# Output products of an attention and SwiGLU block over three PSUM banks instead of two, and turns of h in the bank that stands idle

## The chip, the cores and the metric

The kernel runs on one core of one Trainium2 chip. The metric is the device time of one execution in microseconds, taken as the median of several runs. The profile is one more execution, recorded by the hardware profiler. Its times are counted from the start of its span.

## The reference

One block of a transformer with conditioned layer norms is computed, for 2048 rows of 576 columns. Six vectors of shift, gain and gate come from a condition `c`. Attention has 32 query heads over 16 key and value heads; of the 2048 keys only the last 512 are used, and nothing is masked. The MLP has 4608 inner columns.

```python
mod = (_silu(c) @ w_mod).reshape(c.shape[0], 6, 1, -1)
h = _layernorm(x) * (1 + ca) + sa
q = (h @ wq).reshape(B, Sq, 32, 128).transpose(0, 2, 1, 3)
p = _softmax(einsum("bhqd,bhkd->bhqk", q, k[:, :, -512:]) * 128 ** -0.5)
o = einsum("bhqk,bhkd->bhqd", p, v[:, :, -512:])
x = x + ga * (o.transpose(0, 2, 1, 3).reshape(B, Sq, 4096) @ wo)
h = _layernorm(x) * (1 + cb) + sb
out = x + gb * ((_silu(h @ w1) * (h @ w3)) @ w2)
```

## The kernel before

All engines run in an order that the Python code writes out itself. Each product is made of f16 halves (a high part and a low part), three matmuls for one.

Attention goes through 128 slots, one for a query head and a block of 512 rows; the index is `i`. A slot has four steps `t`, one for 128 of its rows, so a step (i, t) is the unit of the order. In a step TensorE makes the scores of 128 rows against 512 keys (`scores`, L513, three matmuls of 512 columns into tile `pss`), a third of the next slot's query (`query`, L440 and L444, into `pq`; none at t = 3), and one piece of an older pair's output product. At t = 1 it also turns the last quarter of the slot before (`turn`, L554, into `pt`), and after t = 3 it multiplies the slot before by its values (`values`, L593, twelve matmuls into `po`). VectorE finds the exponents (L517), ScalarE takes the exponential (L531) and GpSimd the low halves (L568). The other three quarters of each slot are turned by DMA.

The output product of a pair of heads is `attend_out`. Each of four row tiles of 128 rows is one unit: `back` (L463) is called for head 0 in one step and for head 1 in the next, each time with six matmuls of 128x288, and after the second VectorE adds the sum to the residual: `acc` (L623, 128x576, one instruction over both halves). Units begin at even t and end at odd t. All units of the attention stage use the same two PSUM banks, the tile `E` (in the profile `pe`), columns 0 to 287 of each; small sums over peaks stand in columns 400 to 416 of its second bank (L333, L338, L1174, L1180).

PSUM has eight banks of 512 f32 columns: two for tag A (`pq`, `po`, in the MLP `py`), two for S (`pss`, `px`), two for `E`, two for T (`pt`). The T banks hold the turned quarter of each slot, and now and then a turn of normalised rows (`turn_rows`, L258, four transposes into one bank): those of h for the blocks 1, 2 and 3 before their first use (`make_h`, read by ScalarE in `modulate`, L267, L269, L271, L273), and those of the second norm's h for the blocks 0 and 1 (`store_h`, read by ScalarE, L662). `make_h` runs for blocks 2 and 3 at the steps (8, 0), (8, 1), (8, 2), (9, 0), (9, 1) and (11, 0) to (12, 1); `store_h` runs at (112, 0) to (113, 1) and (115, 0) to (116, 1) in the same pattern. Two rows of shift and gain (`mod_cols`, L170) and a scaling (`scale_cols`, L1108, at (110, 1)) also use T, and the gates (`mod_rows`, L182) use `E`. Tasks of a step (`run(i, t)`) come after its piece of output product.

Block 1's h is made during the first slot (`make_h` with `early`), block 0's ahead of it (`modulate_first`, L285 and L287, from five turned banks, two of them T). The first query goes into `E` (`project_first`, L450 to L456).

When attention ends, the T banks are given back and become a second pair `pf`; from then on `pe` and `pf` take turns (`lane`). The MLP has 72 groups of seven products (L880) and the down products (L965, added by VectorE at L959).

The waits between engines are put in by the tile framework from the tiles that each instruction names.

Of the kernel before, what the change touches and what calls it, by code (L numbers as in the profile page):

```python
# [20 lines left out]
P = 128  # L21
D = 576
DC = 4
# [25 lines left out]
def tile_block(  # L49
# [30 lines left out]

    E = psum.tile([P, 2, 512], F32, tag="E", name="pe", bufs=1)
    turning = ExitStack()
    tpool = turning.enter_context(tc.tile_pool(name="tpool", bufs=2, space=PSUM))

    def t_bank():
        return tpool.tile([P, 512], F32, tag="T", name="pt")

# [73 lines left out]
    def mod_cols(wm, name, one, tag):  # L161

        ps = t_bank() if tag == "T" else bank(tag, f"ps_{name}")
# [12 lines left out]
    def mod_rows(wm, kind):  # L176

        vec = gate_rows[kind]
        wm = wm[0]
        for h in range(2):  # L180
            for d in (0, 3):
                nc.tensor.matmul(  # L182
                    E[:, h, :HALF], ones, wm[:, d, h * HALF : (h + 1) * HALF], start=d == 0, stop=d == 3
                )
        nc.vector.tensor_copy(half_split(vec), E[:, :, :HALF])
        return vec
# [67 lines left out]
    def turn_rows(b, m, tag):  # L254

        ps = t_bank() if tag == "T" else bank(tag, "ps_n")
        for t in range(ST):
            nc.tensor.transpose(ps[:, t * P : (t + 1) * P], norms[b][1][t][:, m * P : (m + 1) * P], ident)  # L258
        return ps
# [70 lines left out]
    def sum_peaks(g, lo, hi, ps=None):  # L330

        ps = E[:, 1, 400:416] if ps is None else ps
        nc.tensor.matmul(ps[:, lo:hi], peak_ones, tops[g][:, lo:hi], start=True, stop=True)  # L333

    def take_sums(g, lo, hi, ps=None):

        ps = E[:, 1, 400:416] if ps is None else ps
        nc.vector.tensor_copy(peaks[g][:, 5 + lo : 5 + hi], ps[:, lo:hi])  # L338
# [118 lines left out]

    def back(ps, o, w, t, first, last):

        rows = slice(t * P, (t + 1) * P)  # L460
        for n, (x, y) in enumerate(((0, 0), (0, 1), (1, 0))):
            for h in range(2):
                nc.tensor.matmul(  # L463
                    ps[:, h, :HALF],
                    o[:, x, rows],
                    w[:, y, h * HALF : (h + 1) * HALF],
                    start=first and n == 0,
                    stop=last and n == 2,
                )

    QP = (range(0, 5), range(5, 10), range(10, 14))
# [13 lines left out]
    def query(i, part):  # L485
        u, j, b = slots[i]
        st = state[i]
        if part == 0 or i == 0:
            st["q"] = bank("A", "pq") if i else E[:, 0, :]
        ps = st["q"]  # L490
        if i == 0:
            project_first(ps, wqs[u, j], hT[b])
        else:
            project(ps, wqs[u, j], hT[b], QP[part])
        if part == len(QP) - 1:
            q = st["qT"] = pool.tile([P, 2, SB], F16, tag=("qh", "ql")[i % 2], name="qT", bufs=QB)
# [51 lines left out]
    def turn(i, t):  # L548

        st = state[i]  # L550
        p = st.pop(("p", t))
        ps = st["t"] = t_bank().rearrange("p (j n) -> p j n", j=KC)
        for j in range(KC):
# [60 lines left out]

    def attend_out(pair, t, j, total):
        u, _, b = slots[2 * pair]
        lane[0] += j == 0
        ps = spare()
        back(ps, state[2 * pair + j]["o"], wos[u][:, j], t, j == 0, j == 1)
        if j == 1:  # L620
            run(*total)
            a = half_split(acc[b][:, t, :])
            nc.vector.scalar_tensor_tensor(  # L623
                a, ps[:, :, :HALF], factors[:, uses[u][0], 2:3], a, op0=ALU.mult, op1=ALU.add
            )
# [29 lines left out]
    def store_h(b, m, tag, tag_out):  # L655
# [8 lines left out]
        )  # L664
        store_later(hd[b][m * P : m * P + n, :], hf[:n], ("s", b, m) if tag == "T" else None)

# [266 lines left out]
    def down(d, u):  # L933

        pair = d // G
        lane[0] += 1
        ps = lane[1][lane[0] % 2]
        if u < 4:
# [28 lines left out]
    def plain(j, i, t):  # L967

        d = 2 * G - 1
        lane[0] += 1  # L970
        ps = lane[1][lane[0] % 2]
        w = osets[d, 3 if j else 4]
# [181 lines left out]

    lane = [0, ()]

    def spare():
        return lane[1][lane[0] % 2] if lane[1] else E

    def in_peak(f, part):  # L1160
# [8 lines left out]
    def in_total(f):  # L1169

        m = peak_cols[:, 4 * (f % 2) :][:, :4]
        for part in range(2):
            peak = m[:, 2 * part + 1 : 2 * part + 2]
            nc.tensor.matmul(  # L1174
                spare()[:, 1, 408:410], peak.to_broadcast([P, P]), m[:, 2 * part : 2 * part + 2],
                start=part == 0, stop=part == 1,
            )

    def in_taken(f):
        nc.vector.tensor_copy(stats[:, f, :], spare()[:, 1, 408:410])  # L1180

# [23 lines left out]
    def out_total(p):  # L1205
        nc.tensor.matmul(spare()[:, 1, 410:411], peak_ones, peak_cols[:, 8 + p % 2 : 9 + p % 2], start=True, stop=True)

    def out_taken(p):
        nc.vector.tensor_copy(out_down[:, p : p + 1], spare()[:, 1, 410:411])

# [235 lines left out]
    def make_h(b, m, early=False):  # L1446
        modulate(hT[b], m, turn_rows(b, m, "T"), vecs["shift", "a"], vecs["gain", "a"], early)

# [86 lines left out]
    at(14, 2, lambda: scale_gate("b", mlp_small, mlp_gate_down))  # L1535
    at(106, 2, make_cols, "shift", "b", 3, 0.0, "T")
    at(109, 2, make_cols, "gain", "b", 4, 1.0, "T")
# [71 lines left out]
    for i in range(n + 2):  # L1609
        run(i, -1)  # L1610
        for t in range(ST):
# [121 lines left out]
```

## Time and profile before

| | |
|---|---|
| median of 3 runs | 2750.64 us (2748.8 to 2751.75) |
| the profiled execution: its own time | 2750.74 us |
| its span on the core | 2748.9 us |
| mean granted TensorE clock | 0.997 |
| TensorE matmul busy | 2678.7 us |
| VectorE, ScalarE, GpSimd busy | 1943.0, 1622.0, 1874.0 us |
| attention, from the first to the last output product | 89 to 1616 us |

PE is TensorE's matmuls, PEld its weight loads, DVE VectorE, ACT ScalarE, POOL GpSimd, SP the engine whose queue issues most DMAs. A group's row gives the line, engine and operation, the tiles out<-in, the shapes and the count, then busy microseconds and mean nanoseconds of one, then the idle time of the engine just ahead of them and what ended it. In the timeline a row begins with its start and its length. A wait's row gives the total, how often, and the longest.

### The profile page before, as it was taken

Reading aid. Unit: us, or ns where it says so; the run is one execution under the profiler, and the core shown is the slowest. Engines: PE = TensorE matmul, PEld = TensorE weight load, DVE = VectorE, ACT = ScalarE, POOL = GpSimd, SP = SyncE. Lnnn points to the kernel's source line nnn. Section 1 sums busy time; section 2 is a strip of 40 time slices with the busy share of each in tenths; the row PEclk is TensorE's granted clock in tenths of the full one; section 3 lists DMA queues with packets and bytes.
Section 4 is the critical chain, followed back from the end, with each engine's and each line's share of the span. In section 5 each row is a group of like instructions: output and inputs, shape, how many; then the busy total and the mean of one; then the engine's idle time right before and its main releaser. Section 6 shows DMA issues by size and latency. Waiting matters only on the chain. (4 is left out here: it accounts for less than half of the span.)

```text
span 2748.9 us, 45218 instructions
## 1 busy us (share of the span) xinstructions
PE 2678.7 (97%) x15406; PEld 1510.3 (55%) x15406; DVE 1943.0 (71%) x3582; ACT 1622.0 (59%) x3026; POOL 1874.0 (68%) x1747
## 2 busy tenths in 40 slices
PE   6899999999999999999999999999999999999998
PEld 3455555555555555555555555555555555555555
DVE  7876777777777777877765567777776666566566
ACT  6776778777777778787677635544443333333332
POOL 4677888888888877877669536688874455333435
PEclk9999999999999999999999999999999999999999
DMA  6888888788787878879879945656643444333332
GB/s 200 184 175 196 184 182 186 176 188 187 167 181 170 190 186 211 200 179 212 187 192 226 224 137 169 201 168 200 209 151 111 153 122 128 106 102 112 104 109 81
DMA packets 593463, 463.87 MB, mean 169 GB/s; under 512 B 442704, under 2 KB 472528, under 8 KB 592208
## 3 DMA queue, kind: packets, MB, share of 16 engines
q1 hardware_dynamic: 592944, 460.69, 66.1%
q8 instruction: 121, 1.98, 0.3%
q14 instruction: 110, 0.90, 0.1%
q10 hardware_dynamic: 288, 0.30, 0.0%
HBM read 264.19 MB, written 95.99 MB: 131 GB/s over the span
## 5 line engine op out<-in xcount | busy, mean ns | idle before, releaser
L568 POOL TENSOR_TENSOR hp<-p,hp 128x512 f16<-128x512 f32 x384 | 447.6, 1168 | 267.0 <-ACT hp L563 154.5
L531 ACT ACTIVATE p<-pss,table,factors 128x512 f32<-128x512 f32 x512 | 396.8, 775 | 351.2 <-DVE table L517 182.4
L517 DVE CUSTOM_DVE_ANT_0 spent<-pss,factors 128x512 uint8<-128x512 f32 x512 | 381.2, 745 | 237.6 <-PE pss L513 236.2
L880 PEld LDWEIGHTS <-wset 128*128 128x128 f16 x3528 | 344.2, 98 | 337.2 <-issue 3.7
L880 PE MATMUL py<-hset,wset 128*128 128x512 f16 x2016 | 482.1, 379 | 0.0
L463 PE MATMUL pe<-o 128*128 128x288 f16 x3024 | 453.0, 286 | 10.6 <-DVE acc L623 10.3
L513 PE MATMUL pss<-k,qT 128*128 128x512 f16 x1536 | 417.7, 380 | 15.3 <-ACT p L531 13.0
L463 PEld LDWEIGHTS <-o 128*128 128x128 f16 x3072 | 300.4, 98 | 184.8 <-issue 16.3
L593 PE MATMUL po<-ptw,v 128*128 128x512 f16 x1536 | 357.1, 381 | 8.8 <-DMA ptw<-hp 2.7
L880 PE MATMUL px<-hset,wset 128*128 128x512 f16 x1512 | 361.5, 379 | 2.2 <-ACT p L531 2.2
L94 POOL TENSOR_TENSOR akv<-u,akv 128x512 f16<-128x512 f32 x141 | 165.2, 1181 | 178.0 <-ACT akv L93 170.2
L440 PE MATMUL pq<-hT,wq 128*128 128x512 f16 x1092 | 280.5, 379 | 0.0
L563 ACT CAST hp<-p 128x512 f16<-128x512 f32 x384 | 237.4, 618 | 15.5 <-DMA ptw<-hp 2.3
L593 PEld LDWEIGHTS <-v 128*128 128x128 f16 x1536 | 147.6, 98 | 174.6 <-issue 13.0
L513 PEld LDWEIGHTS <-qT 128*128 128x128 f16 x1536 | 147.3, 98 | 129.3 <-issue 17.4
L965 PEld LDWEIGHTS <-akv 128*128 128x128 f16 x1728 | 169.0, 98 | 89.3 <-issue 0.7
L623 DVE SCALAR_TENSOR_TENSOR acc<-pe,factors,acc 128x576 f32<-128x576 f32 x252 | 204.2, 810 | 13.0 <-PE pe L463 5.1
L613 POOL TENSOR_TENSOR o<-on,o 128x512 f16<-128x512 f32 x128 | 149.7, 1170 | 54.6 <-ACT o L612 52.2
L440 PEld LDWEIGHTS <-wq 128*128 128x128 f16 x1092 | 106.9, 98 | 127.2 <-issue 1.0
L959 DVE SCALAR_TENSOR_TENSOR acc<-pf,table,acc 128x576 f32<-128x576 f32 x140 | 113.5, 811 | 79.3 <-PE pf L965 79.3
L1058 ACT COPY u<-py 128x512 f32<-128x512 f32 x72 | 42.2, 586 | 200.8 <-PE py L880 198.8
L1051 ACT ACTIVATE s<-s,table 128x512 f32<-128x512 f32 x72 | 52.0, 722 | 175.6 <-DVE s L1050 175.6
(254 smaller groups left out, 4734.2 us busy)
## 6 DMA issues: line engine op xcount, KB each, us to landing
wset<-wd SPq DMA_DIRECT2D x213, 320.0 KB, 3.2
r<-row SPq DMA_DIRECT2D x128, 256.0 KB, 3.9
oset<-od SPq DMA_DIRECT2D x106, 288.0 KB, 3.2
wraw<-in_w SPq DMA_DIRECT2D x36, 768.0 KB, 5.4
wd<-wmade SPq DMA_DIRECT2D x75, 320.0 KB, 3.5
wset<-wd SPq DMA_DIRECT2D x71, 160.0 KB, 2.2
w2raw<-in_w SPq DMA_DIRECT2D x19, 576.0 KB, 5.2
wd<-ring SPq DMA_DIRECT2D x33, 320.0 KB, 2.7
```

The source lines that it names most:

```text
L94: eng.tensor_sub(halves[:, 1], src, halves[:, 0])
L440: nc.tensor.matmul(ps, w[:, k // 2, m, :], hT[:, DC + m if k == 1 else m, :], start=s == 0, stop=False)
L463: nc.tensor.matmul(ps[:, h, :HALF], o[:, x, rows], w[:, y, h * HALF : (h + 1) * HALF], start=first and n == 0, stop=last and n == 2,)
L513: nc.tensor.matmul(pss, q[:, x, rows], k[:, y, :], start=n == 0, stop=n == 2)
L517: nc.vector.tensor_tensor_reduce(spent, pss, to_log.to_broadcast([P, W]), turned, 3.0e38, op0=ALU.add, op1=ALU.min, accum_out=nm)
L531: nc.scalar.activation(p, pss, AF.Exp, bias=nm, scale=factor, accum_out=st["l"][:, t : t + 1])
L563: nc.scalar.copy(hp[:, 0, :], state[i]["p", t])
L568: nc.gpsimd.tensor_sub(hp[:, 1, :], state[i].pop(("p", t)), hp[:, 0, :])
L593: nc.tensor.matmul(po, v[:, x, c, :], pt[:, y, c, :], start=c == 0 and n == 0, stop=c == KC - 1 and n == 2)
L623: nc.vector.scalar_tensor_tensor(a, ps[:, :, :HALF], factors[:, uses[u][0], 2:3], a, op0=ALU.mult, op1=ALU.add)
L880: nc.tensor.matmul(ps, w[:, a, :], h[:, b, :], start=start and n == 0, stop=stop and n == 6, skip_group_check=True)
L965: nc.tensor.matmul(ps[:, h, :HALF], a[:, rows], w[:, b, :], start=m == 0, stop=m == 2)
```

## The change

The tile `E` now has three banks, and T one. A unit of the output product uses two neighbouring banks of `E`: banks 0 and 1 or banks 1 and 2, in turn (`lane` 0 or 1). Its first part makes one half (288 columns) of both heads in the outer bank, its second part the other half in the middle bank; then VectorE reads both. For the first row tile of a pair the last of the six terms moves from the first part to the second. The turns of h, `mod_cols` and `scale_cols` go through `idle()`, the outer bank that the current unit doesn't use; the early turns take banks 0 and 1 by `m % 2`, and the first query takes bank 2. The small sums move to bank 2. The gate of the MLP is made one step later, at (14, 2) instead of (14, 1). When attention ends, the four banks of `E` and T are given back and two new pairs `pe` and `pf` stand in for them.

```diff
-    E = psum.tile([P, 2, 512], F32, tag="E", name="pe", bufs=1)
     turning = ExitStack()
-    tpool = turning.enter_context(tc.tile_pool(name="tpool", bufs=2, space=PSUM))
-
-    def t_bank():
-        return tpool.tile([P, 512], F32, tag="T", name="pt")
+    tpool = turning.enter_context(tc.tile_pool(name="tpool", bufs=1, space=PSUM))
+    E = tpool.tile([P, 3, 512], F32, tag="E", name="pe")
+    lane = [1, ()]
+
+    def both_halves():
+        banks = lane[1][lane[0]] if lane[1] else E[:, lane[0] : lane[0] + 2]
+        return banks[:, :, :HALF]
+
+    def idle():
+        return E[:, 2 - 2 * lane[0], :]
+
+    def spare():
+        return lane[1][lane[0]][:, 1] if lane[1] else E[:, 2]
...
-        ps = t_bank() if tag == "T" else bank(tag, "ps_n")
+        ps = idle() if tag == "E" else E[:, int(tag), :] if tag in "012" else bank(tag, "ps_n")
...
-            st["q"] = bank("A", "pq") if i else E[:, 0, :]
+            st["q"] = bank("A", "pq") if i else E[:, 2, :]
...
-        ps = st["t"] = t_bank().rearrange("p (j n) -> p j n", j=KC)
+        ps = st["t"] = tpool.tile([P, KC, P], F32, tag="T", name="pt")
...
-    def attend_out(pair, t, j, total):
+    TERMS = tuple((j, x, y) for j in range(2) for x, y in ((0, 0), (0, 1), (1, 0)))
+
+    def attend_out(pair, t, part, total):
         u, _, b = slots[2 * pair]
-        lane[0] += j == 0
-        ps = spare()
-        back(ps, state[2 * pair + j]["o"], wos[u][:, j], t, j == 0, j == 1)
-        if j == 1:
+        if not part:
+            lane[0] = 1 - lane[0]
+        now, last = lane[0], [(lane[0], TERMS[-1])] if t == 0 else []
+        if part:
+            jobs = last + [(1 - now, term) for term in TERMS]
+        else:
+            jobs = [(now, term) for term in TERMS[: len(TERMS) - len(last)]]
+        for h, (j, x, y) in jobs:
+            nc.tensor.matmul(
+                both_halves()[:, h],
+                state[2 * pair + j]["o"][:, x, t * P : (t + 1) * P],
+                wos[u][:, j, y, h * HALF : (h + 1) * HALF],
+                start=(j, x, y) == TERMS[0],
+                stop=(j, x, y) == TERMS[-1],
+            )
+        if part:
             run(*total)
             a = half_split(acc[b][:, t, :])
             nc.vector.scalar_tensor_tensor(
-                a, ps[:, :, :HALF], factors[:, uses[u][0], 2:3], a, op0=ALU.mult, op1=ALU.add
+                a, both_halves(), factors[:, uses[u][0], 2:3], a, op0=ALU.mult, op1=ALU.add
             )
...
-        modulate(hT[b], m, turn_rows(b, m, "T"), vecs["shift", "a"], vecs["gain", "a"], early)
+        modulate(hT[b], m, turn_rows(b, m, str(m % 2) if early else "E"), vecs["shift", "a"], vecs["gain", "a"], early)
...
-            at(i + 1 + m // 3, m % 3, store_h, b, m, "T", "raw")
+            at(i + 1 + m // 3, m % 3, store_h, b, m, "E", "raw")
...
-    at(14, 1, make_gate, "b", 5)
+    at(14, 2, make_gate, "b", 5)
...
-    at(110, 1, lambda: scale_cols("b", t_bank(), mlp_small, 2.0**-8))
+    at(110, 1, lambda: scale_cols("b", idle(), mlp_small, 2.0**-8))
...
-    turned = [turn_rows(0, m, "TTAAS"[m]) for m in range(DC + 1)]
+    turned = [turn_rows(0, m, "01AAS"[m]) for m in range(DC + 1)]
...
-                    lane[1] = (E, after.tile([P, 2, 512], F32, tag="T2", name="pf"))
+                    lane[1] = tuple(after.tile([P, 2, 512], F32, tag=tag, name=tag) for tag in ("pe", "pf"))
```

What the instructions wait for is shown with each row: the semaphore's name begins with the engine that raises it.

On TensorE, the beginning of a unit in the middle of attention, before: the end of a query, then head 0's first matmuls.

```order
L440 LDWEIGHTS wq
L440 MATMUL pq<-hT,wq 128x512
L463 LDWEIGHTS o
L463 MATMUL pe<-o 128x288 [waits DVE_49]
L463 LDWEIGHTS o
```

The same place now.

```order
L449 LDWEIGHTS wq
L449 MATMUL pq<-hT,wq 128x512
L623 LDWEIGHTS o
L623 MATMUL pe<-o 128x288 [waits DVE_49]
L623 LDWEIGHTS o
```

The first matmul of a unit's first part goes into another bank than before, and it has a wait on VectorE as before.

On TensorE, the turn of h at step (8, 1) and what follows it, before. It stands behind a unit's last matmul, and the next unit begins behind a query.

```order
L463 LDWEIGHTS o
L463 MATMUL pe<-o 128x288
L258 MATMUL pt<-ident,xn 128x128 [waits Activation_49]
L258 MATMUL pt<-ident,xn 128x128 x3
L513 LDWEIGHTS qT
```

The same place now, and then the beginning of the next unit behind that query.

```order
L623 LDWEIGHTS o
L623 MATMUL pe<-o 128x288
L267 MATMUL pe<-ident,xn 128x128 [waits DVE_49]
L267 MATMUL pe<-ident,xn 128x128 x3
L509 LDWEIGHTS qT
```

```order
L453 LDWEIGHTS wq
L453 MATMUL pq<-hT,wq 128x512
L623 LDWEIGHTS o
L623 MATMUL pe<-o 128x288 [waits Activation_49]
L623 LDWEIGHTS o
```

The turn stands where it stood. Its tile is `pe` now and its wait is on VectorE; the next unit's first matmul waits for ScalarE.

On TensorE, the early turns of h for block 1 at step (0, 3) and the one ahead of step (1, 0), before: the second, third and fourth of five.

```order
L258 MATMUL pt<-ident,xn 128x128 x4
L258 MATMUL pt<-ident,xn 128x128 [waits DVE_49,PE_49]
L258 MATMUL pt<-ident,xn 128x128 x3
L258 MATMUL pt<-ident,xn 128x128 [waits Activation_49]
L258 MATMUL pt<-ident,xn 128x128 x3
```

The same place now.

```order
L267 MATMUL pe<-ident,xn 128x128 [waits DVE_49]
L267 MATMUL pe<-ident,xn 128x128 x3
L267 MATMUL pe<-ident,xn 128x128 [waits Activation_49]
L267 MATMUL pe<-ident,xn 128x128 x3
L267 MATMUL pe<-ident,xn 128x128 [waits Activation_49]
L267 MATMUL pe<-ident,xn 128x128 x3
```

Each of the three turns has a wait now, the third and fourth on ScalarE. On the other engines the instructions stand in the order that they had.

More of the change, by code (lines that the diff above doesn't have):

```diff
@@ L161, in mod_cols @@
     def mod_cols(wm, name, one, tag):
-        ps = t_bank() if tag == "T" else bank(tag, f"ps_{name}")
+        ps = idle() if tag == "E" else bank(tag, f"ps_{name}")
         wm = wm[0]
@@ L179, in mod_rows @@
         wm = wm[0]
+        ps = E[:, 1 - lane[0] : 3 - lane[0], :HALF]
         for h in range(2):
@@ L182, in mod_rows @@
                 nc.tensor.matmul(
-                    E[:, h, :HALF], ones, wm[:, d, h * HALF : (h + 1) * HALF], start=d == 0, stop=d == 3
+                    ps[:, h], ones, wm[:, d, h * HALF : (h + 1) * HALF], start=d == 0, stop=d == 3
                 )
-        nc.vector.tensor_copy(half_split(vec), E[:, :, :HALF])
+        nc.vector.tensor_copy(half_split(vec), ps)
         return vec
@@ L330, in sum_peaks @@
     def sum_peaks(g, lo, hi, ps=None):
-        ps = E[:, 1, 400:416] if ps is None else ps
+        ps = E[:, 2, 400:416] if ps is None else ps
         nc.tensor.matmul(ps[:, lo:hi], peak_ones, tops[g][:, lo:hi], start=True, stop=True)
     def take_sums(g, lo, hi, ps=None):
-        ps = E[:, 1, 400:416] if ps is None else ps
+        ps = E[:, 2, 400:416] if ps is None else ps
         nc.vector.tensor_copy(peaks[g][:, 5 + lo : 5 + hi], ps[:, lo:hi])
@@ L456, in project_first @@
                     nc.tensor.matmul(ps, w[:, k, DC, :], hT[:, 2 * DC, :], start=False, stop=False)
[L458 to L469, printed above, removed]
     QP = (range(0, 5), range(5, 10), range(10, 14))
@@ L664, in store_h @@
         )
-        store_later(hd[b][m * P : m * P + n, :], hf[:n], ("s", b, m) if tag == "T" else None)
+        store_later(hd[b][m * P : m * P + n, :], hf[:n], ("s", b, m) if tag == "E" else None)
     def combine_tiles(pair):
@@ L935, in down @@
         pair = d // G
-        lane[0] += 1
-        ps = lane[1][lane[0] % 2]
+        lane[0] = 1 - lane[0]
+        ps = lane[1][lane[0]]
         if u < 4:
@@ L969, in plain @@
         d = 2 * G - 1
-        lane[0] += 1
-        ps = lane[1][lane[0] % 2]
+        lane[0] = 1 - lane[0]
+        ps = lane[1][lane[0]]
         w = osets[d, 3 if j else 4]
@@ L1153, in tile_block @@
     nc.gpsimd.memset(odd_cols, 1.0)
-    lane = [0, ()]
-    def spare():
-        return lane[1][lane[0] % 2] if lane[1] else E
     def in_peak(f, part):
@@ L1174, in in_total @@
             nc.tensor.matmul(
-                spare()[:, 1, 408:410], peak.to_broadcast([P, P]), m[:, 2 * part : 2 * part + 2],
+                spare()[:, 408:410], peak.to_broadcast([P, P]), m[:, 2 * part : 2 * part + 2],
                 start=part == 0, stop=part == 1,
@@ L1179, in in_taken @@
     def in_taken(f):
-        nc.vector.tensor_copy(stats[:, f, :], spare()[:, 1, 408:410])
+        nc.vector.tensor_copy(stats[:, f, :], spare()[:, 408:410])
     def power_of(up, d, down):
@@ L1205, in out_total @@
     def out_total(p):
-        nc.tensor.matmul(spare()[:, 1, 410:411], peak_ones, peak_cols[:, 8 + p % 2 : 9 + p % 2], start=True, stop=True)
+        nc.tensor.matmul(spare()[:, 410:411], peak_ones, peak_cols[:, 8 + p % 2 : 9 + p % 2], start=True, stop=True)
     def out_taken(p):
-        nc.vector.tensor_copy(out_down[:, p : p + 1], spare()[:, 1, 410:411])
+        nc.vector.tensor_copy(out_down[:, p : p + 1], spare()[:, 410:411])
     def out_scale(p):
@@ L1533, in tile_block @@
             at(i, min(d, ST - 1), weigh, k, d)
-    at(14, 1, make_gate, "b", 5)
-    at(14, 2, lambda: scale_gate("b", mlp_small, mlp_gate_down))
-    at(106, 2, make_cols, "shift", "b", 3, 0.0, "T")
-    at(109, 2, make_cols, "gain", "b", 4, 1.0, "T")
+    at(14, 2, make_gate, "b", 5)
+    at(14, 3, lambda: scale_gate("b", mlp_small, mlp_gate_down))
+    at(106, 2, make_cols, "shift", "b", 3, 0.0, "E")
+    at(109, 2, make_cols, "gain", "b", 4, 1.0, "E")
     at(109, 3, lambda: spread_peaks("b", mlp_small))
-    at(110, 1, lambda: scale_cols("b", t_bank(), mlp_small, 2.0**-8))
+    at(110, 1, lambda: scale_cols("b", idle(), mlp_small, 2.0**-8))
     for piece in range(6):
```

## The prediction

> **What bounds the kernel now.** First the page: the span and each engine's busy time.
>
> ```profile
> span 2748.9 us, 45218 instructions
> PE 2678.7 (97%) x15406; PEld 1510.3 (55%) x15406; DVE 1943.0 (71%) x3582; ACT 1622.0 (59%) x3026; POOL 1874.0 (68%) x1747
> ```
>
> TensorE is busy for 97% of the span and no other engine for more than 71%. So the time is TensorE's matmuls plus 70 us in which it stands, and a change of order is worth what it does to those 70 us. Next the waits of TensorE: total, times, longest.
>
> ```profile
> PE pss L513 <- ACT p L531: 13.0, 17, 2.4
> PE pe L463 <- DVE acc L623: 10.3, 14, 2.0
> PE pe L463 <- DVE us L338: 0.2, 1, 0.2
> ```
>
> The second row is the wait that the three banks speak to: a unit of the output product can't begin while VectorE still adds the unit before, and only 14 of 256 units lose time so. The third row is small and says more. L338 copies sums from columns 400 to 416 of the second bank; L463 writes columns 0 to 287. The two touch no common column, and for its first half (first bank) not even a common bank, yet the first matmul waited. So the program guards the tile `pe` as a whole.
>
> **The waits that the change leaves.** In the changed program a unit's first matmul still carries a wait on VectorE (the first pair of order pieces). I followed each to the instruction that raises it: in 239 of 256 units it is the addition of the unit just before, or a small copy right behind it, as in the kernel before. The outer bank that the matmul writes isn't one of the two that this addition reads, but all three banks are one tile. So the 10.3 us stay: gain 0.
>
> What the two orders of matmuls cost is read from the groups. The second row is a product of the MLP that already makes three matmuls in a row into one bank.
>
> ```profile
> L463 PE MATMUL pe<-o 128*128 128x288 f16 x3024 | 453.0, 286 | 10.6 <-DVE acc L623 10.3 <-DVE us L338 0.2
> L965 PE MATMUL pe<-oset,akv 128*128 128x288 f16 x864 | 129.4, 286 | 0.0
> L554 PE MATMUL pt<-ident,p 128*128 128x128 f32 x512 | 76.9, 273 | 0.0
> ```
>
> 453.0 / 3024 and 129.4 / 864 are both 0.150 us, so alternating banks or staying in one costs the same: 0. The last row is the turn that keeps T. It comes once in four steps and its bank has been read two steps earlier, so one T bank is enough; its new waits are on TensorE's own work of a slot ago: 0. The first part now needs the second head's high half one step sooner. ScalarE makes it before the exponential whose bank TensorE needs for that step's scores, so it is there: 0. The last term, which needs GpSimd's half, has been moved to the second part for that reason.
>
> **Turns at odd steps.** At t = 1 the turn of h comes right behind a unit's last matmul, and its tile is now the one that the addition of that unit reads. It waits for the whole addition. There are eight such turns (steps 1 of slots 8, 9, 11, 12, 112, 113, 115, 116) and the scaling at (110, 1). First, scaling and last of the nine in the timeline of before:
>
> ```profile
> 139.62 0.60 PE L258 MATMUL pt<-ident,xn 128*128 128x128 f32 x4
> 139.82 0.82 DVE L623 SCALAR_TENSOR_TENSOR acc<-pe,factors,acc 128x576 f32<-128x576 f32 x1
> ...
> 1362.88 0.38 PE L1108 MATMUL pt<-spread,ones 128*128 128x128 f32 x2
> 1363.08 0.82 DVE L623 SCALAR_TENSOR_TENSOR acc<-pe,factors,acc 128x576 f32<-128x576 f32 x1
> ...
> 1437.45 0.60 PE L258 MATMUL pt<-ident,xn 128*128 128x128 f32 x4
> 1437.65 0.82 DVE L623 SCALAR_TENSOR_TENSOR acc<-pe,factors,acc 128x576 f32<-128x576 f32 x1
> ```
>
> Each turn began 0.20 us ahead of an addition of 0.82 us, so it comes 1.02 us later. How long a released matmul takes to start is seen where one waited:
>
> ```profile
> 574.77 0.79 DVE L623 SCALAR_TENSOR_TENSOR acc<-pe,factors,acc 128x576 f32<-128x576 f32 x1
> 575.62 0.90 PE L463 MATMUL pe<-o 128*128 128x288 f16 x6 [1.41 <-DVE acc L623]
> 577.60 0.69 DVE L583 TENSOR_TENSOR ptw<-pt,ptw 128x512 f16<-128x512 f32 x1
> 577.79 2.44 PE L593 MATMUL po<-ptw,v 128*128 128x512 f16 x10
> ```
>
> 575.62 - (574.77 + 0.79) = 0.06 us. So 1.08 us each, 9 x 1.08 = 9.7 us (9.2 without the release, 9.9 where a small copy stands behind the addition, as at two of them). Behind the turn TensorE has only its own later steps, and the scores of the next step feed all others: nothing hides it.
>
> **Parts behind a turn.** After each of the twenty turns of that kind the next part of the output product must wait until ScalarE has read the turned bank, though it writes another. Mostly ScalarE is done in time. At five places it isn't: the part's start in before, and ScalarE's read.
>
> ```profile
> 143.39 0.90 PE L463 MATMUL pe<-o 128*128 128x288 f16 x6
> 144.18 0.77 ACT L273 ACTIVATE hf<-pt,mod_a 128x512 f32<-128x512 f32 x1
> ...
> 178.55 0.90 PE L463 MATMUL pe<-o 128*128 128x288 f16 x6
> 179.13 0.77 ACT L273 ACTIVATE hf<-pt,mod_a 128x512 f32<-128x512 f32 x1
> ...
> 180.51 0.90 PE L463 MATMUL pe<-o 128*128 128x288 f16 x6
> 181.77 0.77 ACT L273 ACTIVATE hf<-pt,mod_a 128x512 f32<-128x512 f32 x1
> ...
> 1390.82 0.90 PE L463 MATMUL pe<-o 128*128 128x288 f16 x6
> 1391.43 0.77 ACT L662 ACTIVATE hf<-pt,shift_b,gain_b 128x512 f32<-128x512 f32 x1
> ...
> 1428.33 0.90 PE L463 MATMUL pe<-o 128*128 128x288 f16 x6
> 1429.77 0.77 ACT L662 ACTIVATE hf<-pt,shift_b,gain_b 128x512 f32<-128x512 f32 x1
> ```
>
> The wait is the read's end plus 0.06, less the part's start and the delay that TensorE already has there: 1.08 us, at the third 1.41. If ScalarE stays where it was, that makes 0.54, 0.33, 0.68, 0.36 and 1.19, together 3.1 us. If ScalarE is itself moved by TensorE's delay, which its exponential does wait for, each is up to 1.08 more, at the third 1.41: 8.8 us in all. At the second and third ScalarE is busy with weights and stays; at the others I take half: 1.1 + 0.3 + 0.7 + 0.9 + 1.7 = 4.7 us.
>
> **The gate's step.**
>
> ```profile
> 214.60 2.21 PE L182 MATMUL pe<-wm,ones 128*128 128x288 f32 x8 [0.91 <-DVE acc L623]
> 216.84 0.76 DVE L185 COPY gate_b<-pe 128x576 f32<-128x576 f32 x1 [2.30 <-PE pe L182]
> ```
>
> One step later the addition is over, so 0.91 us go. The copy of 0.76 us then stands ahead of the unit's second part, with only three score matmuls between: some 0.3 us come back. Net -0.6 us (-0.9 to -0.1).
>
> **The start.** The first query goes into the tile from which block 0's h is read, and the early turns follow each other in one tile instead of two.
>
> ```profile
> 23.61 2.12 PE L450 MATMUL pe<-hT,wq 128*128 128x512 f16 x8 [0.74 <-ACT hT L287]
> 25.45 0.79 ACT L287 ACTIVATE hf<-pt,mod_a 128x512 f32<-128x512 f32 x1
> 28.91 0.92 PE L453 MATMUL pe<-hT,wq 128*128 128x512 f16 x3 [0.76 <-POOL hT L296]
> ...
> 41.80 1.11 PE L258 MATMUL pt<-ident,xn 128*128 128x128 f32 x4 [2.74 <-ACT hT L271]
> 42.95 0.81 DVE L267 TENSOR_SCALAR hf<-pt,mod_a 128x512 f32<-128x512 f32 x1 [1.30 <-PE pt L258]
> 43.79 0.78 ACT L271 ACTIVATE hT<-pt,mod_a 128x512 f16<-128x512 f32 x1 [1.33 <-DVE hf L267]
> ```
>
> The query can't begin before ScalarE's second reading of `pt` ends at 26.24, 2.6 us later. Its last three matmuls waited for GpSimd until 28.91 anyway, so at full clock it is nearly hidden; at half clock its 14 matmuls, of some 0.43 us each (twice the step of the L593 row, ten in 2.44 us), end 2.5 us later. I take 1.5 (0 to 2.5). Among the early turns the fourth stood at 41.80 behind the second's read. Now the third stands there, and the fourth behind the third's reads, which take what the last two rows show: it starts at 43.79 + 0.78 + 0.06 = 44.63, 2.8 us later (2.3 to 3.3 by the clock). Some of it may vanish in waits up to 94 us. Together 4.3 us (1.0 to 5.8).
>
> **The clock.** TensorE's granted clock falls for a window where it stood long in the one before: length, busy time of PE, PEld, DVE, ACT, POOL, then the clock.
>
> ```profile
> 37.76:41.17 3.41, 0.63 (x4) 0.42 (x4) 3.41 (x7) 2.19 (x5) 2.42 (x3) 1.00 1.03 214
> 1532.80:1536.21 3.41, 1.42 (x10) 0.86 (x9) 2.76 (x5) 0.90 (x2) 3.41 (x4) 1.00 1.12 230
> 1536.21:1539.62 3.41, 3.41 (x13) 1.49 (x12) 3.38 (x6) 2.53 (x6) 3.32 (x4) 0.50 1.78 130
> ```
>
> Two of 3.41 us idle were enough for a window at half, up to 1.7 us of work lost. The new waits move the 1536 one against its window: it may go, or another come. I count 0 for it, and 1.7 us either way in the range. The Trainium skill ("TensorE: Matmul & The Clock Gate", Part 1) has the window free-running, 3413 ns long, and the clock halved after an idle window. The rows agree on the length; on the condition they differ, for 1.42 us of that window were busy, and the measurement decides. By the page's condition the waits added here, taken at no more than 1.7 us each, would halve nothing; the query's 1.5 us would go, and the sum would be near 16.6 us.
>
> **The sum.** 0 + 9.7 + 4.7 - 0.6 + 4.3 = 18.1 us. The profiled execution took 2750.74 us (span and 1.84 us around it), 0.1 us over the median. 2750.7 + 18.1 = 2768.8, so 2769 us. By the bounds 9.2 + 3.1 - 0.9 + 1.0 = 12.4 and 9.9 + 8.8 - 0.1 + 5.8 = 24.4; with a half window either way 10.7 to 26.1.
>
> **Rivals.** *The wait goes after all, faster.* If a unit's first part does start while VectorE adds the unit before, the 10.3 us are at stake. At 575 us above, though, the values' third matmul, 0.43 us into its group, needs VectorE's L583, which ended at 578.29 whatever TensorE did: those 1.4 us come straight back. If this holds for all, nothing is won; if for this alone, 8.9; and turns wait for no addition. About 2746 us. It decides where the first matmul starts before the addition ends. The third wait row and the wait in the order speak against it: 0.05. The Trainium skill ("PSUM — Partial Sum Buffer", PSUM bank collisions raise a hardware error) says to guard by bank and quadrant. By that rule the outer bank would need no wait; the row of L338 shows a coarser guard in this program, and no run here shows the finer one.
>
> *The added waits are covered.* If TensorE loses at the turns what it would have lost a little later, only a few us are left: 2754 us. But in the slots 8 to 12 and 111 to 116 it hardly waits, and it is 97% busy: 0.05.
>
> *More half clocks.* Four of the pairs of waits in one window, four times 1.7: 2776 us. They lie 3 to 5 us apart, so few share a window: 0.12.
>
> **How the numbers follow.** The forecast has 0.78. A measurement of this kernel can tell about 0.2% (5.5 us) from no change. Faster has the first rival, 0.05; same the second, 0.05; slower the rest, 0.90. The range 2760 to 2777 takes in the bounds and the half clocks; left out are the other two and the tails.
>
> **What would show it.** Right: `pe` on L623 still waits some 10 us in about 14 places for the addition; L267 waits about 1.1 us for it in eight places and the scaling once; L623 waits for ScalarE's L282 or L672 some five times; the query at 24 us starts behind 26 us, and the MLP is as long as before. Wrong: no wait on L623's first matmul, turns that start beside the addition, or a start no later than before.

## The result, and the profile after

The changed kernel takes 2767.41 us (2766.78 to 2768.33, 6 runs), the kernel before 2750.21 us on the same chip (2747.59 to 2751.75, 6 runs). The ratio is 1.0066, its 95% interval 1.0055 to 1.0076: slower by 17 us, where 18 were forecast.

The page of the changed kernel first: the span is 17.0 us longer, and TensorE still busy for 97% of it.

```profile
span 2765.9 us, 45341 instructions
PE 2683.9 (97%) x15406; PEld 1512.3 (55%) x15406; DVE 1942.7 (70%) x3582; ACT 1622.8 (59%) x3026; POOL 1870.6 (68%) x1747
```

TensorE's waits after (total, times, longest). L623 is the product's matmul (L463 before), L267 a turn of h or of the early x (L258), L633 the addition (L623), L459 the first query (L450).

```profile
PE pe L623 <- DVE acc L633: 8.6, 13, 1.7
PE pe L267 <- DVE acc L633: 6.0, 6, 1.1
PE pe L267 <- ACT hT L280: 4.6, 2, 2.8
PE pe L459 <- ACT hf L296: 3.1, 1, 3.1
...
PE pe L623 <- ACT hf L672: 2.7, 2, 1.7
...
PE pe L623 <- ACT hf L282: 1.7, 2, 1.0
PE pe L267 <- DVE table L1185: 1.1, 1, 1.1
...
PE pe L623 <- DVE us L347: 1.1, 1, 1.1
...
PE pe L267 <- DVE us L347: 1.1, 1, 1.1
...
PE pe L1118 <- DVE acc L633: 0.9, 1, 0.9
```

The first row is the wait that three banks were to end: 8.6 us in 13 places, against 10.3 in 14. One unit waits besides for a small copy (L623 for L347), 1.1 us where it was 0.2. The second row, the two rows in which a turn waits for a small copy (L1185 and L347 stand right behind an addition) and the scaling (L1118) are the nine added waits for VectorE, 6.0 + 1.1 + 1.1 + 0.9 = 9.1 us. The rows of L672 and L282 are the parts that wait for ScalarE's read of a turned bank, 4.4 us. The rest is the start.

One turn and the part behind the next, slot 8, in the timeline:

```profile
146.33 0.82 DVE L633 SCALAR_TENSOR_TENSOR acc<-pe,factors,acc 128x576 f32<-128x576 f32 x1
...
147.20 0.66 PE L267 MATMUL pe<-ident,xn 128*128 128x128 f32 x4 [0.98 <-DVE acc L633]
...
149.82 0.60 PE L267 MATMUL pe<-ident,xn 128*128 128x128 f32 x4
...
151.25 0.77 ACT L282 ACTIVATE hf<-pe,mod_a 128x512 f32<-128x512 f32 x1
...
152.08 1.02 PE L623 MATMUL pe<-o 128*128 128x288 f16 x7 [1.01 <-ACT hf L282]
```

146.33 + 0.82 + 0.05 = 147.20: the turn starts when the addition is over. 151.25 + 0.77 + 0.06 = 152.08: the part starts when the read is over, though it writes the unit's own outer bank and the middle one, and the turn lies in the third.

Where the time goes is best seen by a mark that every version has: the turn of the weights into T, once in a slot at step 1. The table gives how much later it starts than in the trace of before, in us, for all profiles of this study; the last column is the difference of the spans. (The expectations number these marks from nought, one lower than here.)

```
slot            5      8     14     15    109    118    128    end
changed       6.4    6.4   14.1   13.2   11.8   20.4   16.7   17.0
repeat        7.3    8.2   15.9   15.1   14.5   23.1   21.1   21.4
order         3.0    3.0    2.9    2.9    3.5    3.6   -0.8   -0.9
start         2.2    2.2   10.2    9.4    9.2   17.8   14.5   13.6
query         2.1    2.2    9.3    8.5    7.4   16.0   15.2   14.3
ahead         7.4    7.4   13.9   13.1   11.8   17.4   15.5   14.0
tbank         5.1    7.0   12.7   11.9   10.8   22.0   17.9   16.4
halves        3.9    4.4   12.2   11.4   19.2   28.5   24.1   23.4
split        -1.5   -0.2    1.6    0.4    4.1    5.6    2.2    1.1
early        -1.2   -1.1    0.3   -0.9   -7.1   -4.3   -9.0  -10.5
two          -1.4   -1.3   -1.1   -2.3   -6.0   -4.7   -7.8   -8.9
```

For the changed kernel: the start 6.4, the turns of slots 8 to 13 7.6, the gate -0.8, the middle -1.4, the scaling and the turns of slots 110 to 117 8.6, the last ten slots -3.7, the MLP 0.4.

The MLP's largest group reads as in the kernel before (482.1 us, 379 ns there too):

```profile
L890 PE MATMUL py<-hset,wset 128*128 128x512 f16 x2016 | 482.1, 379 | 0.0
```

### The profile page after: what moved, and what is told of

Read it like the earlier page. It is cut to its first block, busy times and chain, and to the rows that moved or that the text cites. A ratio compares the mean times of both kernels' runs of the same rounds, so it can differ in the third digit from the quotient of the medians.

```text
span 2765.9 us, 45341 instructions
## 1 busy us (share of the span) xinstructions
PE 2683.9 (97%) x15406; PEld 1512.3 (55%) x15406; DVE 1942.7 (70%) x3582; ACT 1622.8 (59%) x3026; POOL 1870.6 (68%) x1747
## 5 line engine op out<-in xcount | busy, mean ns | idle before, releaser
L890 PE MATMUL py<-hset,wset 128*128 128x512 f16 x2016 | 482.1, 379 | 0.0
L623 PE MATMUL pe<-o 128*128 128x288 f16 x3024 | 452.1, 286 | 15.7 <-DVE acc L633 8.6
L509 PE MATMUL pss<-k,qT 128*128 128x512 f16 x1536 | 417.8, 380 | 16.2 <-ACT p L527 14.3
L623 PEld LDWEIGHTS <-o 128*128 128x128 f16 x3072 | 300.1, 98 | 189.7 <-issue 23.2
L559 ACT CAST hp<-p 128x512 f16<-128x512 f32 x384 | 237.3, 618 | 13.5 <-DMA ptw<-hp 0.5
L633 DVE SCALAR_TENSOR_TENSOR acc<-pe,factors,acc 128x576 f32<-128x576 f32 x252 | 204.2, 810 | 17.8 <-PE pe L623 9.2
L969 DVE SCALAR_TENSOR_TENSOR acc<-pe,table,acc 128x576 f32<-128x576 f32 x140 | 113.6, 811 | 79.2 <-PE pe L975 79.2
```

The costliest lines, as they stand in the source:

```text
L509: nc.tensor.matmul(pss, q[:, x, rows], k[:, y, :], start=n == 0, stop=n == 2)
L559: nc.scalar.copy(hp[:, 0, :], state[i]["p", t])
L623: nc.tensor.matmul(both_halves()[:, h], state[2 * pair + j]["o"][:, x, t * P : (t + 1) * P], wos[u][:, j, y, h * HALF : (h + 1) * HALF], s ...
L633: nc.vector.scalar_tensor_tensor(a, both_halves(), factors[:, uses[u][0], 2:3], a, op0=ALU.mult, op1=ALU.add)
L890: nc.tensor.matmul(ps, w[:, a, :], h[:, b, :], start=start and n == 0, stop=stop and n == 6, skip_group_check=True)
```

## The experiments

All ratios are to the kernel before, timed on the same chip. In the theory the guard over the whole tile `pe` makes every added wait and keeps the old one.

**The order of the matmuls alone.** The kernel before, with a half at even and a half at odd steps in its two banks:

```diff
-        back(ps, state[2 * pair + j]["o"], wos[u][:, j], t, j == 0, j == 1)
...
+        now, last = lane[0] % 2, [(lane[0] % 2, TERMS[-1])] if t == 0 else []
+        if part:
+            jobs = last + [(1 - now, term) for term in TERMS]
+        else:
+            jobs = [(now, term) for term in TERMS[: len(TERMS) - len(last)]]
...
+                spare()[:, h, :HALF],
```

> The kernel before with the new order of the output product's matmuls alone: one half at even steps, the other at odd steps, in two banks as before; turns of h in the two banks of T, the start and the gate as before. Theory (the order costs nothing): 2750 us, within 2 us. Rival (it costs by itself: the second head's high half is needed a step sooner, or matmuls in a row into one bank are slower): 2754 or more.

Measured: 2751.48 us, ratio 1.0002 (0.9993 to 1.0010). No change that can be told, as the theory has it. Its waits for the addition are 8.6 us in 13 places, as in the changed kernel:

```profile
PE pe L613 <- DVE acc L623: 8.6, 13, 1.5
```

So the 1.7 us between 10.3 and 8.6 don't come from the third bank: most of it is a wait of 1.29 us at 1574.57 us in the kernel before, which is gone here too. The table has a warning besides: this kernel's start is that of the kernel before, and yet it stands 3.7 us later in slot 3, ahead of its first output product, and 3.0 in slot 5. With that go more half-clock windows, below.

**Three tiles of one bank.** The guard by bank, with nothing else changed but that the addition (and the copy of a gate) needs two instructions:

```diff
-    E = tpool.tile([P, 3, 512], F32, tag="E", name="pe")
+    E = [tpool.tile([P, 512], F32, tag=f"E{k}", name="pe") for k in range(3)]
...
-            nc.vector.scalar_tensor_tensor(
-                a, both_halves(), factors[:, uses[u][0], 2:3], a, op0=ALU.mult, op1=ALU.add
-            )
+            for h in (now, 1 - now):
+                nc.vector.scalar_tensor_tensor(
+                    a[:, h], one_half(h), factors[:, uses[u][0], 2:3], a[:, h], op0=ALU.mult, op1=ALU.add
+                )
```

> The changed kernel with its three banks as three tiles of one bank each; the addition becomes two of 288 columns, one for each bank, since one instruction can't span two tiles. The guard over the whole tile is then gone. Theory (the guard over all of `pe` makes the waits): in the profile of the changed kernel the turns' and the scaling's waits for VectorE (6.0 + 1.1 + 1.1 + 0.9 = 9.1 us), the parts' waits for ScalarE's reads (2.7 + 1.7 = 4.4), the start (some 6) and the units' waits for the addition (8.6) all hang on it. The first three go: 2767 - 9 - 4 - 6 = 2748 us. Of the 8.6 us some comes straight back in a later wait: between 2740 and 2748, taken 2744. VectorE has some 0.2 us more for each unit, beside TensorE's work: 0. Rival 1 (the units' waits are hidden anyway): 2748, no faster than the kernel before. Rival 2 (the loss comes from the new order of the matmuls or the single T bank, not from the guard): it stays at 2760 or more.

Measured: 2754.27 us, ratio 1.0010 (1.0002 to 1.0019). The nine added waits for VectorE are gone, as expected, the four for ScalarE too, and 13 us with them; below the kernel before, where the forecast put it, it doesn't come. Its waits:

```profile
PE pss L509 <- ACT p L527: 18.4, 24, 2.4
PE po L589 <- DVE ptw L579: 6.5, 12, 0.7
...
PE pe L623 <- ACT hf L282: 1.4, 2, 1.2
PE pe L623 <- ACT hf L673: 1.3, 2, 0.7
...
PE pe L623 <- DVE acc L634: 1.2, 2, 1.1
```

The wait for the addition fell from 8.6 to 1.2 us, and `p` rose from 14.3 to 18.4, `ptw` from 1.1 to 6.5: 7.4 us went and 9.5 came. The two rows of `hf` are new places: 0.19, 1.24, 0.60 and 0.69 us, each behind a turn at an odd step. There the next part opens a unit in the very bank that was turned, and a guard by bank has to wait for ScalarE's read. The place at 587 us in the changed kernel, and the same place here:

```profile
586.56 0.80 DVE L633 SCALAR_TENSOR_TENSOR acc<-pe,factors,acc 128x576 f32<-128x576 f32 x1
...
587.41 0.77 PE L623 MATMUL pe<-o 128*128 128x288 f16 x5 [1.43 <-DVE acc L633]
```

```profile
574.86 0.78 PE L623 MATMUL pe<-o 128*128 128x288 f16 x5
...
575.59 0.92 DVE L634 SCALAR_TENSOR_TENSOR acc<-pe,factors,acc 128x288 f32<-128x288 f32 x2
...
576.12 0.29 PE L623 MATMUL pe<-o 128*128 128x288 f16 x1
...
576.56 0.90 PE L623 MATMUL pe<-o 128*128 128x288 f16 x6 [0.15 <-DVE acc L634]
...
578.02 0.18 PE L1180 MATMUL pe<-peak_cols 128*128 128x2 bf16 x1 [0.56 <-DVE peak_cols L1171]
...
579.28 2.32 PE L589 MATMUL po<-ptw,v 128*128 128x512 f16 x10 [0.57 <-DVE ptw L579]
```

The unit's first part (574.86) no longer waits, and its last matmul (576.12) starts during the additions; only the six into the middle bank, which the addition reads, wait. But 1.43 us of wait became 0.15 + 0.56 + 0.57 = 1.28: VectorE is late there, and TensorE meets it a little later. The prediction's first rival named this return for the place at 575 us of the kernel before. What the trace of before could not show was the price of the second addition, so it was run by itself.

**Two additions, one tile.** The changed kernel with the second edit above alone.

> The changed kernel with each unit's addition made in two instructions of 288 columns, one for each bank, and the three banks still one tile: what the kernel with one-bank tiles paid for its guard, without the guard. Theory (VectorE's second addition is on the path where VectorE is late): the waits for the addition grow from 8.6 us to 11 to 13 and those for `p` and `ptw` grow by some 4; 2772 us (2769 to 2776). Rival (the second addition costs nothing, and the one-bank tiles gained little for another reason): 2767, within 1 us.

Measured: 2778.44 us, ratio 1.0099 (1.0087 to 1.0112): 11 us over the changed kernel, 9 over its repeat on the same chip (2769.52 us, below), about twice what was expected. The waits grew by less than that: 10.7 us for the addition, 16.1 for `p` and 1.9 for `ptw`, together 4.7 more than in the changed kernel. The addition in the changed kernel and here:

```profile
L633 DVE SCALAR_TENSOR_TENSOR acc<-pe,factors,acc 128x576 f32<-128x576 f32 x252 | 204.2, 810 | 17.8 <-PE pe L623 9.2 <-ACT p L527 0.3 <-PE pe L342 0.2
```

```profile
L634 DVE SCALAR_TENSOR_TENSOR acc<-pe,factors,acc 128x288 f32<-128x288 f32 x504 | 235.6, 509 | 17.1 <-PE pe L623 9.4 <-PE pe L342 0.2 <-PE pe L1180 0.2
```

VectorE has 31.4 us more work, on an engine that is busy for 71%. Between slots 15 and 109 alone this kernel falls 9.2 us behind the changed one (11.4 to 19.2 in the table, against 13.2 to 11.8); one half-clock window, from 804.38 us, is among them. This run is also the fair partner of the one before: with the same additions, the guard by bank is worth 2778.44 - 2754.27 = 24 us.

**The additions spread.** With one-bank tiles the first half can be added a step earlier:

```diff
+        soon = t != 0 and not lane[1]
         if part:
             run(*total)
+            halves_done = (1 - now,) if soon else (now, 1 - now)
+        else:
+            halves_done = (now,) if soon else ()
+        for h in halves_done:
...
```

> The kernel with one-bank tiles, the addition of the first half moved to right behind the first part, a step earlier, at three of four rows of tokens (at the first its last term comes with the second part). Theory (the units' waits for the addition came back as waits for `p` and `ptw` because VectorE had two additions in a row at odd steps): with one addition at each step `p` falls back from 18.4 to 14 or 15 us and `ptw` from 6.5 to 2 or 3: 2754 - 7 = 2747 us (2744 to 2750). Rival (what VectorE does in all decides, or the addition at even steps now delays the low halves of the turned weights): 2753 or more.

Measured: 2744.24 us, ratio 0.9979 (0.9970 to 0.9989): faster than both kernels. The wait for `ptw`:

```profile
PE po L589 <- DVE ptw L579: 4.9, 8, 1.3
```

The wait for `p` fell from 18.4 to 12.7 us, below the changed kernel's 14.3; that for `ptw`, 6.5 before, fell less than expected. Of the waits of a product's matmul for an addition one of 0.3 us is left. VectorE does more here than in the kernel before, 1985.3 us against 1943.0, at times when less waits for it: not its sum decides, but what stands in its queue when TensorE needs it.

**Without the third bank.** The same in the kernel before: two tiles of one bank, first half always first, two banks for the turns.

```diff
+    E = [tpool.tile([P, 512], F32, tag=f"E{k}", name="pe", bufs=1) for k in range(2)]
...
+            jobs = last + [(1, term) for term in TERMS]
...
+            ready = (1,) if soon else (0, 1)
```

> The kernel before with what made the last version faster and without a third bank: its two banks as two tiles of one bank, always the first half at even steps and the second at odd steps, each half added right behind its part (at the first of four rows of tokens both behind the second). The turns keep two banks, the start stays as in the kernel before. Theory (the finer guard and the spread additions win the time, the third bank only takes a bank from the turns): the units' waits for the addition are nearly gone, the parts never wait for ScalarE; 2742 us (2738 to 2746). Rival (the alternation over three banks is what frees a unit's first part; with two banks it waits for the addition of a step ago): 2747 or more, with waits for the addition of 5 us or more.

Measured: 2745.54 us, ratio 0.9981 (0.9972 to 0.9991), the same as with three banks. Its product's matmul waits for nothing that counts:

```profile
L614 PE MATMUL pe<-o 128*128 128x288 f16 x3024 | 453.0, 286 | 0.7 <-DVE acc L629 0.4 <-POOL o L601 0.2
```

So the third bank earns nothing that two guarded banks don't, and it is taken from the turns.

**Turns ahead of the unit.** The nine waiters moved to right behind the step's scores:

```diff
                 scores(i, t)
+            run(i, ("ahead", t))
...
-            at(i + 1 + m // 3, m % 3, make_h, b, m)
+            at(i + 1 + m // 3, ("ahead", 1) if m % 3 == 1 else m % 3, make_h, b, m)
```

> The changed kernel with the turns of h at odd steps, and the scaling at (110, 1), moved from behind the unit's second part to right behind the scores of the same step, ahead of that part. No unit stands complete there, so no addition is waited for. Theory: the 9.1 us that these nine waited for VectorE go; the second part behind them now waits where ScalarE has not read the turn in time, 0 to 3 us over eight places: 2767 - 9 + 1.5 = 2759.5 us (2757 to 2762). Rival (what TensorE loses at the turns it would lose a little later in any case): 2764 to 2767.

Measured: 2765.19 us, ratio 1.0050 (1.0037 to 1.0063): 2 us below the changed kernel by the medians, 4 by the ratios, not 8. The forecast failed, the rival is nearer. The nine waits for VectorE are gone from the trace, but others grew:

```profile
PE pe L623 <- ACT hf L282: 3.9, 2, 2.1
PE pe L623 <- ACT hf L672: 3.1, 2, 1.9
...
PE pe L267 <- ACT hf L672: 1.7, 3, 0.6
...
PE pe L267 <- ACT hf L282: 0.6, 1, 0.6
```

Together 9.3 us, against 4.4 in the changed kernel: 4.9 of 9.1 came back. Slot 8 shows how: TensorE comes earlier, but ScalarE, which has an exponential, a cast and a query's copy to do first, doesn't. The wait of 2.13 us lies in a window with 1.28 of 3.41 us busy, and the next window, from 154.11 us, is at half clock.

```profile
150.43 0.60 PE L267 MATMUL pe<-ident,xn 128*128 128x128 f32 x4
...
152.98 0.77 ACT L282 ACTIVATE hf<-pe,mod_a 128x512 f32<-128x512 f32 x1
...
153.81 1.58 PE L623 MATMUL pe<-o 128*128 128x288 f16 x7 [2.13 <-ACT hf L282]
```

**Turns in T's bank.** None of them touches `pe`:

```diff
-        ps = idle() if tag == "E" else E[:, int(tag), :] if tag in "012" else bank(tag, "ps_n")
+        ps = tpool.tile([P, 512], F32, tag="T", name="ph") if tag == "E" else E[:, int(tag), :] if tag in "012" else bank(tag, "ps_n")
...
-            at(i + 1 + m // 3, m % 3, make_h, b, m)
+            at(i + (0, 1, 1, 1, 2)[m], (3, 0, 2, 3, 0)[m], make_h, b, m)
```

> The changed kernel with the turns of h and the scaling at (110, 1) in T's one bank, at the steps when it is free (3 of the slot of the norm, 0, 2 and 3 of the next, 0 of the one after; the scaling at step 2), so that none of them touches `pe`. Theory: the 9.1 us of turns and scaling that waited for VectorE and the 4.4 us of parts that waited for ScalarE go; T's single bank gives 0 to 3 us of waits in their place: 2767 - 13.5 + 1.5 = 2755 us (2753 to 2758). Rival (other waits take their place, as in the kernel with the turns put ahead, where 2 us came of 9): 2761 or more.

Measured: 2773.14 us, ratio 1.0078 (1.0066 to 1.0090), 4 us over the changed kernel's repeat on the same chip, with intervals that overlap; at any rate not the 2755 expected. The waits of the turns and parts that were expected to go did go; in their place:

```profile
PE pt L550 <- ACT hf L672: 5.5, 4, 1.7
...
PE pt L550 <- ACT hf L282: 3.8, 4, 1.1
...
PE ph L267 <- DVE ptw L579: 2.7, 3, 1.1
...
PE ph L267 <- ACT hf L672: 1.1, 1, 1.1
```

With 1.1 for the scaling, 0.9 for another read of `hf` and 0.9 for a normalised row that isn't ready, that is 16.0 us for the 13.5 that went. The estimate of 0 to 3 us for T had left out that the turn of the weights, too, now waits behind a read of h. In the idle bank of the one tile and in T's single bank the turns pay alike; with two banks of T, in the kernel before, the list of waits has none of these.

**The start.** First the query alone in T's bank, then the early turns too, in T and `pe` by turns (the last two lines):

```diff
-            st["q"] = bank("A", "pq") if i else E[:, 2, :]
+            st["q"] = bank("A", "pq") if i else tpool.tile([P, 512], F32, tag="T", name="pq0")
...
-        modulate(hT[b], m, turn_rows(b, m, str(m % 2) if early else "E"), vecs["shift", "a"], vecs["gain", "a"], early)
+        modulate(hT[b], m, turn_rows(b, m, "T0"[m % 2] if early else "E"), vecs["shift", "a"], vecs["gain", "a"], early)
```

> The changed kernel with only the first query moved into T's bank; the early turns of block 1 still follow each other in `pe`. Theory (the start loses in two places, at the query and at the early turns): the query's wait of 3.1 us for ScalarE shrinks to about 1 and the first turn of the weights stands 3 to 4 us behind the kernel before in place of 5.9; the early turns' second wait stays; 2765 us (2763 to 2767), between the changed kernel and the one with its whole start undone. Rival (only the early turns count): 2767 or more.

> The changed kernel with its start undone: the first query goes into the bank of T, and the early turns of block 1 take that bank and one of `pe` by turns. Theory: what the start lost by single file in one tile comes back: up to the fourth slot the changed kernel stands 6.4 us behind the kernel before, by the two traces; 4 to 6 of them go: 2762 us (2761 to 2764). Rival (the half-clock windows at the start of the changed kernel fell there by chance and not by its waits): only 1 to 2 us go, 2765 to 2766.

Measured: 2767.01 us, ratio 1.0058 (1.0045 to 1.0071), for the query; 2764.80 us, ratio 1.0052 (1.0038 to 1.0065), for both. By the times this is inconclusive: the intervals overlap each other and that of the changed kernel, and both medians lie just above the ranges forecast, near the rivals. By the profiles both stand 2.2 us behind before in slot 8, where the changed kernel stands 6.4. The query's wait for ScalarE is gone in the first; the second keeps 0.7 us of it, as much as the kernel before had, shortens the early turns' wait from 4.6 to 2.7, and the weights' turn now meets the last early turn in T:

```profile
PE pe L267 <- ACT hT L280: 2.7, 1, 2.7
...
PE pt L550 <- ACT hT L280: 1.8, 1, 1.8
```

**The changed kernel once more.**

> The changed kernel once more, for a second profile. Theory (the half-clock windows at the start fall as the clock's grid happens to lie): up to the fourth slot it stands 4 to 8 us behind the kernel before's profile, by more than 1 us away from the 6.4 of the first profile if the number of half windows before 100 us is not seven; slots 7 to 13 cost 7.6 us and slots 110 to 117 8.5 us as before, within 0.4. Rival (the windows come from the new waits): seven windows again and 6.4 us within 0.3.

Measured: 2769.52 us, ratio 1.0064 (1.0051 to 1.0077). The turns cost 7.6 and 8.6 us again, as in the first profile. The start did not repeat: 7.3 us in slot 5 and 8.2 in slot 8. The expectation's seven half windows were miscounted: the first profile has eight before 100 us (three from 20.94, two from 44.83, two from 58.48, one from 85.79), this one nine. Another one, from 1598.86 us, falls into its last ten slots, which save 2.0 us here and 3.7 in the first profile.

## Why the prediction was right, point by point

- **The waits that stay: 0.** Right. 8.6 of 10.3 us stayed, and the kernel with the order alone has 8.6 too. That the guard over the whole tile is the cause is shown by the pair with equal additions: 24 us. The Trainium skill ("PSUM — Partial Sum Buffer", PSUM bank collisions raise a hardware error) has the guard by bank and quadrant; with one tile for each bank the traces agree as far as banks go, for at 576.12 us a matmul writes one bank while the additions read the other two, and 1.2 us of that wait are left.
- **Orders and one T bank: 0.** Right for the order (1.0002). For T it is right only because the turns of h had been moved out of it.
- **Turns at odd steps: 9.7.** Right; 9.1 in nine places, 0.9 to 1.1 each. That they stand on the path by themselves was only half right: with the turns put ahead, 4.9 of the 9.1 us came back as waits for ScalarE.
- **Parts behind a turn: 4.7.** Right; 4.4 in four places, 1.01, 0.74, 1.01 and 1.71 where 1.1, 0.7, 0.9 and 1.7 stood; the one of 0.3 didn't show. One statement was too wide: the part writes another bank than the turned one only behind turns at even steps, where all four waits stand. Behind the eight at odd steps it writes that very bank, and there one-bank tiles wait too.
- **The gate: -0.6.** -0.8.
- **The start: 4.3, at most 5.8.** The mechanism was right, the size too small. The first scores before, then query, scores and fourth early turn after:

```profile
30.52 0.60 PE L513 MATMUL pss<-k,qT 128*128 128x512 f16 x2 [0.69 <-ACT qT L497]
```

```profile
26.88 3.57 PE L459 MATMUL pe<-hT,wq 128*128 128x512 f16 x8 [3.11 <-ACT hf L296]
...
32.86 1.12 PE L509 MATMUL pss<-k,qT 128*128 128x512 f16 x3 [0.69 <-ACT qT L493]
...
46.56 1.12 PE L267 MATMUL pe<-ident,xn 128*128 128x128 f32 x4 [1.82 <-ACT hT L280]
```

  The query began behind 26 us, and the first scores came at 32.86 in place of 30.52: 2.3 us, not 1.5; the prediction had 1.5 between full and half clock, and the three windows from 20.94 on were at half clock. The fourth early turn came at 46.56 in place of 41.80: 4.8 us, of which 2.5 are the turns' own (2.8 forecast). The rest up to 6.4 comes while the windows from 44.83 to 51.66 and from 58.49 to 65.31 us are at half clock; how much of it the clock makes isn't shown apart.
- **The clock: 0.** This step failed. It looked at the window at 1536 us, and that one did go; but at the start there were eight half windows where there had been two. How many of them the added waits made isn't shown: the kernel with the order alone, which has none of these waits, had six. The same view after, window by window (length, busy time of PE, PEld, DVE, ACT, POOL, clock):

```profile
17.53:20.94 3.41, 1.28 (x12) 1.09 (x10) 3.16 (x12) 3.35 (x6) 0.00 (x0) 1.00 1.06 392
```

```profile
20.94:24.35 3.41, 2.44 (x8) 1.88 (x9) 2.39 (x9) 3.35 (x9) 2.14 (x6) 0.50 1.07 296
24.35:27.77 3.41, 0.88 (x3) 0.32 (x3) 3.38 (x5) 3.11 (x6) 3.26 (x4) 0.50 0.87 331
27.77:31.18 3.41, 3.41 (x10) 1.18 (x9) 3.28 (x7) 2.13 (x6) 0.93 (x1) 0.50 0.02 7
```

  A window with 1.28 us of 3.41 busy is followed by one at half clock, and so is a half one with 2.44 or 0.88. Over the twelve profiles, from 14 to 2735 us, each full-clock window with up to some 1.46 us of matmuls was followed by a half one (1.46 from 77.08 us in the kernel with the additions spread), and none with 1.77 us or more was (1.77 from 1565.29 us there). Between them it went both ways: 1.49 us from 52.89 us in the kernel with the query moved was not, 1.76 us from 68.00 us in the one with the order alone was. The Trainium skill ("TensorE: Matmul & The Clock Gate", Part 1) asks for an idle window; here, as in the kernel before, none of these was idle.
- **What the sum left out: -5.1.** In the middle -1.4 (small differences of waits), in the last ten slots -3.7: the half window at 1536 us is gone (1.9 with the wait beside it), and so is the wait of 1.29 us at 1574.57 us. The kernel with the order alone loses them too, so they are not the third bank's; the half window may be chance, for the repeat had one in its last ten slots again. They cancel the shortfall at the start (2.1) and in the turns of slots 8 to 13 and 110 to 117 (14.4 forecast, 16.2 by the table): the total was closer than its terms, and that it came within 1 us is luck. Of the 16.2 the waits counted above are 13.5 and a new wait for a transposing DMA at 208 us 0.6. Part of the rest is TensorE's own busy time, which is longer where waits break it (four turned matmuls take 0.66 us behind a wait and 0.60 without, in slot 8 above). The second of the two stretches, before and after, with equal counts of matmuls:

```profile
1346.30:1458.20 111.90, 111.69 (x668) 65.52 (x667) 79.33 (x176) 81.72 (x158) 71.28 (x73) 1.00 0.85 202
```

```profile
1358.10:1478.60 120.50, 112.66 (x668) 65.31 (x666) 79.55 (x176) 81.90 (x157) 71.06 (x73) 1.00 0.79 187
```

  112.66 - 111.69 = 1.0 us over seven waits, 0.14 each, which the forecast of 1.08 a turn did not have.
- **The rivals.** The first, that the wait goes and 1.4 us come back at 575 us, describes the kernel with one-bank tiles, down to the place. The second, that added waits are covered, fell for the changed kernel but came half true when the turns were moved. The third had pairs of added waits at the turns make half windows; none came there, and those that came stand at the start.

What stays open: how much of the start's loss is the order of the work and how much the clock's phase. The two kernels with their start undone in part or whole both stand at 2.2 us in slot 8, with five half windows each before 100 us, but their times can't tell.

## What to carry to other kernels

A bank more can free a wait only if the program guards by bank, and here two banks guarded so did as well as three: look for a wait between instructions that share a tile and no bank (here the small copy in columns 400 to 416), and make one tile of each bank before the order is changed. Where a buffer of two becomes one, list everything that shares it and who reads it, for under three schedules here such waits took 9 to 16 us. When a wait goes, look whose engine was late: here a kernel beat the one before only when that engine's queue was cleared as well, with the additions spread over two steps.

## What the runs showed of the hardware beyond that

The clock's windows lie differently from profile to profile. The first half one starts at 41.17 us in the kernel before, at 23.63 in the one with the order alone, whose start is the same:

```profile
23.63:27.04 3.41, 3.19 (x8) 1.17 (x8) 3.38 (x5) 3.41 (x7) 3.26 (x3) 0.50 1.00 378
```

That start had two half windows in one profile and six in the other, and 3.0 us lay between them in slot 5. So a start read from one profile is uncertain by some 3 us in this kernel (an estimate from these two), more than some terms of the sum.

Two additions of 288 columns back to back took 0.92 us together where one of 576 took 0.80 to 0.82. In the mean each took 509 ns, against 810 for the one.
